# Attention with a routed feed-forward on one core: gathered blocks transposed six half rounds after their gather, the first ranking's steps behind the maximum, weights a round later

## The chip, the cores and the metric

The kernel runs on one core of a Trainium2 chip. The metric is device time in microseconds of that core for one execution. Four engines run side by side: TensorE (PE; its weight loads are PEld), VectorE (DVE), ScalarE (ACT) and GpSimd (POOL); the queue of SyncE (SP) issues most transfers. [...]

## What is computed

Chunked attention: q, k and v have 8 batches, 8 heads, 576 positions and 64 columns; every chunk of 64 positions attends to itself alone. The result, seen as 4608 rows of 512 columns, then goes through a mixture of experts in which only some rows take part, each with its best of 8 experts.

```
scores = scale * np.matmul(q_c, k_c.transpose(0, 1, 2, 4, 3))
scores = scores - np.max(scores, axis=-1, keepdims=True)
attn = np.exp(scores)
attn = attn / (np.sum(attn, axis=-1, keepdims=True) + 1e-09)
x = np.matmul(attn, v_c)                      # as rows of 512

do_compute = (x @ w_skip) > 0
logits = x[do_compute] @ w_gate               # 8 experts
e = argmax(logits);  gate = softmax(logits)[e]
h = np.maximum(x @ w1[e], 0.0)                # 512 -> 1024
out = x + gate * (h @ w2[e])                  # rows that take part; x elsewhere
```

## The kernel before

**Rounds.** The attention works on 36 tiles of 128 rows. One loop, `for i in range(-1, NT + 5)` (line 698), is a software pipeline; I call one pass of it a round and name it by i. Round i issues, in this order on TensorE: the transposes of the probabilities of tile i-1 (`pe_ptrans`, L259), the subtraction of the maximum of tile i (`pe_sub`, L248), the transposes of the attention result of tile i-3 (`pe_xtrans`, L297), a first share of feed-forward work (`fill`, half round 2i), the scores of tile i+1 (`pe_scores`, L237), the gate logits of tile i-4 (`pe_logits`, L322 and L323), the product with v of tile i-1 (`pe_pv`, L276), and a second share of feed-forward work (half round 2i+1). So the row of L237 with tile t belongs to round t-1, and the distance of two such rows is the length of a round.

DVE has in a round: the reduction of the logits (`ve_logits`, L332), the normalisation of tile i-2 (`ve_norm`, L282, L284, L286) and the maximum of tile i+1 (`ve_max`, L242, which waits for the scores of the same round). `pe_logits` writes into the same PSUM tile `pv` that `ve_norm` reads, so L322 of a round waits for L286 of that round. ACT has the exponential (L252), the copy of the transposed probabilities (L264) and the copy of the transposed result (L308); POOL splits that copy into a high and a low float16 part (L309, L312: two halves of 256 columns up to tile 14).

**Ranking.** The 36 tiles fall into five groups of 4, 8, 8, 7 and 9 tiles. When a group's logits are complete, `route(g)` (line 339) turns them into row numbers for each expert's blocks. It is a generator whose steps each carry a kind and a cost: "d" for DVE steps, "p" for the counting matmuls, "r" for reading their result, "w" a pause, "q" for the matmuls that collect the records. `run_route(kinds, budget)` (line 461) issues steps of the kinds named until the costs use the budget up. Line 729 does it ahead of `ve_max`, line 741 behind `pe_pv`. The first group alone (`early()`) has shares of 700 and 600; it fills blocks 0 to 2 of the first expert, 128 rows each. Its last steps are `finish_records` (L443 to L445), which yields the row numbers `reci`.

**Gather and filler.** `early_fetch(True)` then starts one gather a round (`gather`, L490, an indirect transfer that POOL issues, out of the rows that the stores have written to `out`). `filler()` (line 635) is a generator of the first expert's feed-forward on these three blocks: four transposes a block (L503), then layer 1 (L524) and layer 2 (L549), one step at a time. `fill(0.95)` in every half round takes a step if the generator gives one; it gives none until `is_open(m)`, that is until `F_LAG[m]` half rounds after block m's gather (5, 5, 4; 6 for the fourth). After the last tile, what is left of it is taken at once.

**Transfers by a table.** `EXTRAS` says in which round a store (`s`) or a piece of the first expert's weights (`w`, 256 KB) or of the second's (`r`, 512 KB) is issued on SP's queue; `CONV` in which round a piece of weights is split into float16 parts by ACT and POOL (L485 to L487). q, k and v of a tile are loaded about two to three rounds ahead. A tile's store must have landed before its slot of `hold` or `xb` is written again by L286. `more_constants` (line 209) prepares the gate's weights for L322; it stands behind round 3.

After the loop the other experts' blocks follow, unit by unit.

Of the kernel before, what the change touches and what calls it, by code (L numbers as in the profile page):

```python
# [14 lines left out]
ALU = mybir.AluOpType  # L15
# [28 lines left out]
EARLY_G, EARLY_B = 1, 3  # L44
# [5 lines left out]
RS = 5120  # L50
EMPTY = 5120.0

LOOK = 3
EXTRAS = {3: "- s0", 5: "s1", 7: "s2", 8: "s3", 11: "w0", 12: "w1", 13: "w2", 14: "w3", 15: "w4", 16: "w5 s4", 17: "w6 s5", 18: "w7 s6",
# [3 lines left out]
CONV = {i: "w" for i in range(14, 31) if i != 27} | {35: "r", 36: "r", 37: "r", 38: "r", 39: "r", 40: "rrr"}  # L58
HOLD, XB, H_LAST = 8, 6, 26
NPRE = 15  # L60
F_LAG = (5, 5, 4, 6)
F_RATE = 0.95
W_ORDER = tuple((fc, part) for part in range(2) for fc in range(FC))
WSETS = 3
# [43 lines left out]
def moe_attention_kernel(ctx: ExitStack, tc: tile.TileContext, q: bass.AP, k: bass.AP, v: bass.AP, cst: bass.AP, wall: bass.AP, out: bass.AP):  # L108
    nc = tc.nc
# [20 lines left out]
    xb = ap.tile([P, XB, DM], F32, name="xb", bufs=1)  # L130
    store_at = {int(u[1:]): i for i, us in EXTRAS.items() for u in us.split() if u[0] == "s"}
    slots, free_at = [], [-1] * (HOLD + XB)
# [10 lines left out]
    def paced(dma):  # L143
        if pe_last[0] is not None:
            ins, to = (getattr(x, "ins", x) for x in (dma, pe_last[0]))
            tc.add_manual_dep(ins, to.name, mybir.DependencyInfo(mybir.DependencyClass.Sync, mybir.DependencyReason.DATA), reason="transfers are spread over the iteration")

    def load_q(t):
        if t < NT:
            T[t]["qk"] = qkb[:, t % (LOOK + 1)]  # L150
            paced(nc.sync.dma_start(T[t]["qk"][:, 0], q[t]))

    def load_k(t, eng=None):
        if t < NT:
            paced((eng or nc.sync).dma_start(T[t]["qk"][:, 1], k[t]))

    def load_v(t):
        if t < NT:
            T[t]["v"] = vb[:, t % (LOOK + 1)]
            paced(nc.sync.dma_start(T[t]["v"], v[t]))  # L160
# [42 lines left out]
    addr = cpool.tile([P, NT], F32, name="addr")  # L203
# [5 lines left out]
    def more_constants():  # L209
        nc.scalar.activation(wgs[:, :, 0], wg, AF.Copy, scale=SR)  # L210
        nc.gpsimd.tensor_scalar(wg, wg, SR, 1.0, op0=ALU.mult, op1=ALU.mult)
        nc.gpsimd.tensor_tensor(wgs[:, :, 1], wg, wgs[:, :, 0], op=ALU.subtract)

    def row_constants():
        nc.scalar.activation(upper, C("upper"), AF.Copy)
        nc.scalar.activation(iota, C("iota"), AF.Copy)
        nc.gpsimd.tensor_copy(vals[:, :, 0], C("tok"))
        nc.gpsimd.tensor_copy(vals[:, :, 2], C("part").to_broadcast([P, NT]))
        nc.gpsimd.memset(ecum[:, 0, :], 0.0)
        nc.gpsimd.memset(rec, 0.0)  # L220
# [118 lines left out]
    def route(g):  # L339
        n, t0 = GS[g], sum(GS[:g])  # L340
# [16 lines left out]
        val = spool.tile([P, n], F32, name="val", bufs=2)  # L357
# [18 lines left out]
        w = f.stop - f.start  # L376
# [26 lines left out]
        rank = spool.tile([P, n], F32, name="rank", bufs=2)  # L403
        nc.vector.tensor_reduce(rank, ad, axis=AX.X, op=ALU.add)
        if g < CUT_G:
# [6 lines left out]
            yield "d", 100  # L412
            key = spool.tile([P, n], F32, name="key", bufs=2)
            nc.vector.scalar_tensor_tensor(key, val, -40.0, bi, op0=ALU.mult, op1=ALU.add)
        yield "d", 100
        nc.vector.scalar_tensor_tensor(addr[:, t0:t0 + n], val, -float(RS), rank, op0=ALU.mult, op1=ALU.add)
        if g >= CUT_G:
            return
        yield "d", 220
# [16 lines left out]
        nc.vector.tensor_tensor(rec, rec, rp.rearrange("p (z b) -> p z b", z=4), op=ALU.add)  # L436
        if g + 1 == EARLY_G:
            finish_records(0, EARLY_B)
        elif g + 1 == CUT_G:
            finish_records(EARLY_B, NB)  # L440

    def finish_records(lo, hi):
        nc.vector.scalar_tensor_tensor(reci[:, lo:hi], rec[:, 0, lo:hi], EMPTY, rec[:, 2, lo:hi], op0=ALU.add, op1=ALU.add)  # L443
        nc.vector.tensor_tensor(recg[:, lo:hi], rec[:, 1, lo:hi], rec[:, 3, lo:hi], op=ALU.add)  # L444
        nc.vector.tensor_scalar(recg[:, lo:hi], recg[:, lo:hi], 1.0 / (SGATE * SX * SW * SW), None, op0=ALU.mult)  # L445
        ready.append(hi)
# [5 lines left out]
    def late_group():  # L452
        return routes and routes[0][2] >= CUT_G

    def early():
        return routes and routes[0][2] < EARLY_G

    def urgent():
        return routes and routes[0][2] + 1 == CUT_G

    def run_route(kinds, budget):
        while routes and routes[0][0][0] in kinds and budget > 0:
            budget -= routes[0][0][1]
            held[0] = {"p": "p", "q": "q", "r": ""}.get(routes[0][0][0], held[0])
            routes[0][0] = next(routes[0][1], None)
            if routes[0][0] is None:
                routes.pop(0)
# [14 lines left out]
    def conv_half(w_pend):  # L482
        st, fc, r = w_pend.pop(0)
        w = w1x if r is None else wsets[0][:, :, :, r]
        nc.scalar.activation(w[:, 0, fc], st, AF.Copy, scale=SW)  # L485
        nc.gpsimd.tensor_scalar(st, st, SW, 1.0, op0=ALU.mult, op1=ALU.mult)
        nc.gpsimd.tensor_tensor(w[:, 1, fc], st, w[:, 0, fc], op=ALU.subtract)  # L487
# [75 lines left out]
    def on(f, t, *a):  # L563
        if 0 <= t < NT:
            f(t, *a)
# [21 lines left out]
    def early_fetch(mid=False):  # L587
        m = min([m for m in range(EARLY_B) if m not in xgs], default=EARLY_B)
        if m < EARLY_B and cur[0] % 2 == 0 and mid:
            fetch(m, EARLY_ROWS)  # L590
        if ready[-1] == NB:
            m = min([m for m in range(EARLY_B, XGB) if m not in xgs], default=XGB)
            if m < XGB:
                fetch(m, CUT_ROWS)
        for m in xgs:
            fetched.setdefault(m, cur[0])
# [31 lines left out]
    def is_open(m):  # L628
        return m in fetched and cur[0] >= fetched[m] + F_LAG[min(m, EARLY_B)]

# [42 lines left out]
    def fill(n):  # L673
        credit[0] += n
        while credit[0] >= 1 and next(fill_, False):
            credit[0] -= 1
        credit[0] = min(credit[0], 1)

    def flush(n=1 << 30):
        while late and n:  # L680
            f, *a = late.pop(0)
            f(*a)
            n -= 1
# [10 lines left out]
    def move(us):  # L694
        for u in us:
            {"-": int, "s": store, "w": load_half, "r": load_raw}[u[0]](int(u[1:] or 0))

    for i in range(-1, NT + 5):
        cur[0] = 2 * i
        extra = [u for u in EXTRAS.get(i, "").split()]  # L700
        if held[0]:
            run_route("d", 1 << 30)
        run_route("r", 1)
        run_route("w", 1)
        early_fetch()
        on(ve_logits, i - 5)
        on(ve_norm, i - 2)
        on(pe_ptrans, i - 1)
        if i < NPRE:
            on(ac_pt, i - 1)  # L710
        on(pe_sub, i)
        on(ac_exp, i)
        if i >= NPRE:
            on(ac_pt, i - 1)
        if i == 0 or i > 1:
            load_q(i + LOOK + (i == 0))
        on(pe_xtrans, i - 3)
        move(extra[2:])
        on(ac_xt, i - 3, i - 3 >= NT - 9)
        fill(F_RATE if i < NT else 2)  # L720
        if i == 0 or i > 1:
            load_k(i + LOOK + (i == 0))
        on(pe_scores, i + 1)
        if i == 1:
            paced(nc.sync.dma_start(csb, cst))
        move(extra[:1])
        if not urgent() and not early():
            run_route("q", 1)
        run_route("d", 600 if urgent() else 700 if early() else 350 if not late_group() else 0)
        on(ve_max, i + 1)  # L730
        flush()
        on(pe_logits, i - 4, i - 1 if i - 1 < NT else None)
        on(pe_pv, i - 1)
        for t in range(vnext[0], min(NT, i + LOOK) if i >= 0 else 0):
            load_v(t)
            vnext[0] = t + 1
        if urgent() or early():
            run_route("q", 1)
        if not late_group():
            run_route("p", 1)  # L740
        run_route("rd" if urgent() or early() else "d", 600 if urgent() or early() else 200 if not late_group() else 0)
        early_fetch(True)
        cur[0] = 2 * i + 1
        fill(F_RATE if i < NT else 2)
        if i == 3:
            more_constants()
        if i == 5:
            row_constants()
        move(extra[1:2])
        for u in CONV.get(i, ""):  # L750
            conv_half(w_pend if u == "w" else r_pend)
# [141 lines left out]
    for u, (p, bs, offs, n) in list(enumerate(units))[1:]:  # L893
# [10 lines left out]
        w, hc = wsets[p], ht  # L904
# [103 lines left out]
```

## Time and profile before

| what | us |
|---|---|
| median of 3 runs | 336.6 |
| the profiled execution's own time | 336.5 |
| its span, first to last instruction | 334.7 |
| PE busy | 314.5 |
| DVE busy | 235.4 |
| POOL busy | 153.9 |

A row of a timeline gives its start, its length, the engine, the line, what is written and read, and in brackets how long the engine had been idle and who ended that. A timeline merges neighbouring instructions of one line (x32 is 32 of them). A row of windows gives a stretch, its length, the busy time of each engine with the count of its instructions, the granted clock of TensorE, the busy share of the transfer engines and GB/s. Between span and time lie 1.8 us.

### The profile page before, as it was taken

How to read it: one execution, taken by the hardware profiler on the slowest of the kernel's cores; microseconds unless marked ns; L12 is line 12 of the kernel's file. 1: busy time of each engine (PE TensorE's matmuls, PEld its weight loads, DVE VectorE, ACT ScalarE, POOL GpSimd, SP SyncE). 2: the span in 40 equal slices, each digit the busy share in tenths (PEclk: the TensorE clock that was granted, in tenths of full speed). 3: DMA queues.
4: the chain of work that ended last, by engine and by line, in shares of the span. 5: the costliest groups of instructions: out<-in, count | busy, mean ns of one | idle time of the engine just before them, and what ended most of it. 6: DMA issues, size and time to landing. Idle time of an engine off the chain costs nothing. (4 is left out here: it accounts for less than half of the span.)

```text
span 334.7 us, 11279 instructions
## 1 busy us (share of the span) xinstructions
PE 314.5 (94%) x4537; PEld 221.8 (66%) x4537; DVE 235.4 (70%) x558; ACT 163.2 (49%) x340; POOL 153.9 (46%) x190
## 2 busy tenths in 40 slices
PE   7999896999999999999999999999999999999991
PEld 3777675777777777767555447647647649678580
DVE  1656763879478758955579876886887999868430
ACT  2555444655546543354557454554554555457120
POOL 5176685989979780358960451231232221120111
PEclk9999899999999999999999999999999999999997
DMA  7998889899999999969824787666667676754010
GB/s 258 340 316 277 282 247 354 263 301 303 307 318 291 348 388 364 379 213 343 289 65 125 255 307 226 208 209 227 192 220 253 194 224 233 243 172 154 34 30 28
DMA packets 41320, 81.83 MB, mean 245 GB/s; under 512 B 5022, under 2 KB 5022, under 8 KB 41264
## 3 DMA queue, kind: packets, MB, share of 16 engines
q1 hardware_dynamic: 38016, 71.48, 64.3%
q0 software_dynamic: 3104, 9.33, 8.6%
q8 instruction: 37, 0.61, 0.7%
q10 hardware_dynamic: 144, 0.26, 0.2%
q14 instruction: 19, 0.16, 0.1%
HBM read 67.02 MB, written 14.17 MB: 243 GB/s over the span
## 5 line engine op out<-in xcount | busy, mean ns | idle before, releaser
L549 PE MATMUL y<-wset,ht 128*128 128x512 f16 (+7 forms) x480 | 86.2, 380 | 0.0
L490 POOL DMA_INDIRECT out<-yo,reci x22 | 24.5, 1114 | 119.0 <-DVE yo L559 112.6
L524 PEld LDWEIGHTS <-wset 128*128 128x128 f16 x768 | 63.9, 98 | 14.5 <-issue 2.3
L549 PEld LDWEIGHTS <-ht 128*128 128x128 f16 (+7 forms) x552 | 44.8, 101 | 42.4 <-issue 2.0
L802 DVE SCALAR_TENSOR_TENSOR wset<-wst,wset 128x512 f16<-128x512 f32 x96 | 61.5, 683 | 0.8 <-ACT wset L801 0.4
L524 PE MATMUL hp<-xt,wset 128*128 128x288 f16 (+4 forms) x576 | 60.4, 267 | 0.0
L801 ACT ACTIVATE wset<-wst 128x512 f16<-128x512 f32 x96 | 53.9, 620 | 3.9 <-DVE wset L802 2.2
L528 ACT ACTIVATE ht<-hp 128x288 f16<-128x288 f32 (+5 forms) x56 | 21.7, 388 | 44.3 <-PE hp L524 44.1
L242 DVE TENSOR_REDUCE mx<-sp 128x8 bf16<-128x512 f32 x36 | 24.7, 687 | 24.9 <-PE sp L237 24.9
L252 ACT ACTIVATE px<-sp 128x512 f32<-128x512 f32 x36 | 21.4, 595 | 37.3 <-PE sp L248 29.1
L516 DVE SCALAR_TENSOR_TENSOR ht<-hp,ht 128x288 f16<-128x288 f32 (+5 forms) x56 | 23.6, 429 | 17.1 <-ACT ht L528 16.5
L312 POOL TENSOR_TENSOR xh<-xs,xh 128x256 f16<-128x256 f32 (+1 forms) x42 | 33.4, 811 | 2.2
L264 ACT ACTIVATE pts<-pt 128x512 f32<-128x512 f32 x36 | 21.4, 595 | 20.7 <-PE pt L259 20.7
L490 POOL DMA_INDIRECT xg<-out,reci x22 | 24.6, 1116 | 12.2 <-DVE recg L444 6.8
L237 PEld LDWEIGHTS sp<-qkb 64*64 64x64 f32 x1152 | 20.6, 136 | 11.4 <-ACT px L252 7.5
L276 PE MATMUL pv<-vb,pts 64*64 64x65 f32 x1152 | 26.4, 225 | 0.9 <-issue 0.8
L309 POOL CAST xh<-xs 128x512 f16<-128x512 f32 x27 | 16.8, 621 | 21.2 <-ACT xs L308 21.0
L237 PE MATMUL sp<-qkb 64*64 64x64 f32 x1152 | 25.7, 227 | 0.8 <-ACT px L252 0.6
L276 PEld LDWEIGHTS pv<-vb,pts 64*64 64x64 f32 x1152 | 21.1, 135 | 2.2 <-issue 1.4
L504 ACT ACTIVATE xt<-xq 128x512 f16<-128x512 f32 (+6 forms) x18 | 9.1, 511 | 27.6 <-PE xq L503 27.6
L259 PE MATMUL pt<-ident,px 128*128 128x128 f32 x144 | 22.4, 278 | 0.1
L559 DVE SCALAR_TENSOR_TENSOR yo<-y,recg,xg 128x512 f32<-128x512 f32 (+7 forms) x20 | 14.8, 741 | 7.6 <-PEq L944 5.0
(138 smaller groups left out, 463.9 us busy)
## 6 DMA issues: line engine op xcount, KB each, us to landing
wst<-in_wall SPq DMA_DIRECT2D x96, 256.0 KB, 3.9
vb<-in_v SPq DMA_DIRECT2D x36, 260.0 KB, 4.7
qkb<-in_q SPq DMA_DIRECT2D x36, 256.0 KB, 5.0
qkb<-in_k SPq DMA_DIRECT2D x35, 256.0 KB, 5.0
out<-hold SPq DMA_DIRECT2D x20, 256.0 KB, 5.2
wset<-in_wall SPq DMA_DIRECT2D x16, 256.0 KB, 5.2
out<-xb SPq DMA_DIRECT2D x16, 256.0 KB, 5.0
wset<-in_wall SPq DMA_DIRECT2D x8, 512.0 KB, 6.7
```

Of the source, the lines that this page charges most:

```text
L237: pe_last[0] = nc.tensor.matmul(sp[halves[a], c, j * CH:(j + 1) * CH], qk[halves[c], 0, w], qk[halves[c], 1, w], start=(j == 0), stop=Fals ...
L242: nc.vector.tensor_reduce(mx, T[t]["sp"][:, :, :KC * CH].rearrange("p c (j s) -> p c j s", s=CH), axis=AX.X, op=ALU.max, negate=True)
L259: pe_last[0] = nc.tensor.transpose(pt[:, j, :], px[:, j * P:(j + 1) * P], ident)
L276: pe_last[0] = nc.tensor.matmul(pv[halves[c], jj, m * VW:(m + 1) * VW], pt[halves[jj], c * 2 + jp, halves[a]], vv[halves[jj], c * KC + m, ...
L312: nc.gpsimd.tensor_tensor(xh[:, 1, w], xs[:, w], xh[:, 0, w], op=ALU.subtract)
L490: ins = nc.gpsimd.indirect_dma_start(**kw)
L516: nc.vector.scalar_tensor_tensor(ht[:, 1, fc, :n], hp, 0.0, ht[:, 0, fc, :n], op0=ALU.max, op1=ALU.subtract)
L524: pe_last[0] = nc.tensor.matmul(hp, w()[:, a, fc, j * P:(j + 1) * P], xt[:, b, j, :n], start=(m == 0), stop=(m == 11))
L528: nc.scalar.activation(ht[:, 0, fc, :n], hp, AF.Relu)
L549: pe_last[0] = nc.tensor.matmul(y[c * P // cg:c * P // cg + n], ht[:, a, fc, o:o + n], w[:, b, fc, P * KC:], start=(f == 0 and m == 0), st ...
L801: nc.scalar.activation(w[:, 0, fc, r], st[part], AF.Copy, scale=SW)
L802: nc.vector.scalar_tensor_tensor(w[:, 1, fc, r], st[part], SW, w[:, 0, fc, r], op0=ALU.mult, op1=ALU.subtract)
```

## The change

Four things. The three early blocks are transposed six half rounds behind their gather, where it was 5, 5 and 4. The first group's ranking gets no share ahead of the maximum any more; it gets 450 right behind it and 350 behind `pe_pv`, and the step that writes `addr` goes to the end, behind `finish_records`. The gate's weights are prepared behind round 2, not 3. The first expert's weights are loaded and split a round later, and some stores are put elsewhere in the table.

```
-EXTRAS = {3: "- s0", 5: "s1", 7: "s2", 8: "s3", 11: "w0", 12: "w1", 13: "w2", 14: "w3", 15: "w4", 16: "w5 s4", 17: "w6 s5", 18: "w7 s6",
...
+EXTRAS = {3: "- s0", 5: "s1", 7: "s2", 9: "s3", 12: "w0", 13: "w1", 14: "w2", 15: "w3", 16: "w4 s4", 17: "w5 s5", 18: "w6 s6", 19: "w7 s7",
...
-CONV = {i: "w" for i in range(14, 31) if i != 27} | {35: "r", 36: "r", 37: "r", 38: "r", 39: "r", 40: "rrr"}
+CONV = {i: "w" for i in range(15, 32) if i != 28} | {35: "r", 36: "r", 37: "r", 38: "r", 39: "r", 40: "rrr"}
...
-F_LAG = (5, 5, 4, 6)
+F_LAG = (6, 6, 6, 6)
...
-        yield "d", 100
-        nc.vector.scalar_tensor_tensor(addr[:, t0:t0 + n], val, -float(RS), rank, op0=ALU.mult, op1=ALU.add)
+        def address():
+            nc.vector.scalar_tensor_tensor(addr[:, t0:t0 + n], val, -float(RS), rank, op0=ALU.mult, op1=ALU.add)
+
+        if g + 1 != EARLY_G:
+            yield "d", 100
+            address()
...
         if g + 1 == EARLY_G:
             finish_records(0, EARLY_B)
+            yield "d", 100
+            address()
...
-        run_route("d", 600 if urgent() else 700 if early() else 350 if not late_group() else 0)
+        if not early():
+            run_route("d", 600 if urgent() else 350 if not late_group() else 0)
         on(ve_max, i + 1)
+        if early():
+            run_route("d", 450)
...
-        run_route("rd" if urgent() or early() else "d", 600 if urgent() or early() else 200 if not late_group() else 0)
+        run_route("rd" if urgent() or early() else "d", 600 if urgent() else 350 if early() else 200 if not late_group() else 0)
...
-        if i == 3:
+        if i == 2:
             more_constants()
```

On DVE, in round 8, where the first group's ranking begins, from the normalisation (L286) on; m, ex, eq, val, eh and es are the ranking's:

```order
 L286 TENSOR_TENSOR hold<-pv,rr 128x512
+L242 TENSOR_REDUCE mx<-sp 128x8
 L347 TENSOR_REDUCE m<-lg 128x4
 L350 TENSOR_TENSOR ex<-lg,m 128x32
```

```order
 L358 TENSOR_REDUCE val<-eq 128x4
 L360 SCALAR_TENSOR_TENSOR val<-lg,val 128x4
-L242 TENSOR_REDUCE mx<-sp 128x8
 L363 TENSOR_TENSOR eh<-csb,val 128x36
 L366 TENSOR_REDUCE es<-eh 128x9
```

The maximum moves from behind the first five steps to ahead of all seven.

On DVE, rounds 9 to 11 before the change, from the ranking's read of its counts (den, gate, rank, bi, sl, key, addr, ohb and oh are the ranking's):

```order
L392 TENSOR_REDUCE den<-pe 128x4
L397 RECIPROCAL gate<-den 128x4
L332 TENSOR_REDUCE lg<-pv 128x9
L282 TENSOR_SCALAR rs<-pv 128x8
L284 RECIPROCAL rr<-rs 128x8
L286 TENSOR_TENSOR hold<-pv,rr 128x512
L404 TENSOR_REDUCE rank<-ad 128x4
L408 TENSOR_SCALAR bi<-rank 128x4
L411 SCALAR_TENSOR_TENSOR sl<-bi,rank 128x4
L414 SCALAR_TENSOR_TENSOR key<-val,bi 128x4
L416 SCALAR_TENSOR_TENSOR addr<-val,rank 128x4
L421 TENSOR_TENSOR ohb<-csb,key 128x88
```

And the same place of the changed kernel:

```order
L392 TENSOR_REDUCE den<-pe 128x4
L332 TENSOR_REDUCE lg<-pv 128x9
L282 TENSOR_SCALAR rs<-pv 128x8
L284 RECIPROCAL rr<-rs 128x8
L286 TENSOR_TENSOR hold<-pv,rr 128x512
L242 TENSOR_REDUCE mx<-sp 128x8
L397 RECIPROCAL gate<-den 128x4
L404 TENSOR_REDUCE rank<-ad 128x4
L408 TENSOR_SCALAR bi<-rank 128x4
L411 SCALAR_TENSOR_TENSOR sl<-bi,rank 128x4
L414 SCALAR_TENSOR_TENSOR key<-val,bi 128x4
L425 TENSOR_TENSOR ohb<-csb,key 128x88
```

`gate`, which reads what POOL made of `den`, no longer stands ahead of the normalisation; `addr` has left this place.

On PE, rounds 14 to 16 (fb<-ident,xg are the transposes of a gathered block; L503 of before is L509 of the changed kernel); in round 13 one such row has gone as well:

```order
 L276 MATMUL pv<-vb,pts 64x65 x16
-L503 MATMUL fb<-ident,xg 128x128 x4
 L259 MATMUL pt<-ident,px 128x128 x4
 L248 LDWEIGHTS identb
```

```order
 L297 MATMUL xt<-ident,xb 128x128 x4
-L503 MATMUL fb<-ident,xg 128x128 x4
+L509 MATMUL fb<-ident,xg 128x128 x4
 L237 MATMUL sp<-qkb 64x64 x16
```

The three blocks were transposed in half rounds 27, 29 and 30; now it is 30, 32 and 34, always between L297 and L237. Layer 1 of the filler, which began in half round 31, begins in 35.

## Rows read from the trace of the kernel before

**Rows 1.** The page's busy times: engine, busy us, share of the span.

```profile
PE 314.5 (94%) x4537; PEld 221.8 (66%) x4537; DVE 235.4 (70%) x558; ACT 163.2 (49%) x340; POOL 153.9 (46%) x190
```

**Rows 2.** Windows: stretch, length, busy of the five engines, PEclk, DMA share, GB/s.

```profile
36.00:44.00 8.00, 6.60 (x162) 5.55 (x162) 6.07 (x19) 2.85 (x6) 5.04 (x11) 0.79 0.81 262
...
50.00:60.00 10.00, 6.86 (x164) 5.92 (x168) 3.59 (x9) 5.59 (x11) 6.44 (x9) 1.00 0.90 324
60.00:80.00 20.00, 19.39 (x447) 15.38 (x438) 17.67 (x50) 11.08 (x24) 17.54 (x24) 1.00 0.94 298
...
52.00:54.00 2.00, 1.37 (x48) 1.04 (x45) 0.17 (x1) 1.51 (x4) 0.88 (x2) 1.00 1.04 398
```

**Rows 3.** Timeline of PE, rounds 4 to 19: start, length, what, idle before.

```profile
18.08 0.17 PE L322 MATMUL pv<-wgs,xh 128*128 128x18 f16 x1 [0.52 <-POOL wgs L212]
...
30.08 0.69 PE L237 MATMUL sp<-qkb 64*64 64x64 f32 x32
32.87 0.69 PE L237 MATMUL sp<-qkb 64*64 64x64 f32 x32
33.50 0.18 PE L322 MATMUL pv<-wgs,xh 128*128 128x18 f16 x1
...
37.64 0.17 PE L322 MATMUL pv<-wgs,xh 128*128 128x18 f16 x1 [0.98 <-DVE hold L286]
39.94 0.58 PE L248 MATMUL sp<-mx,identb 128*128 128x256 bf16 x2 [0.35 <-DVE mx L242]
41.31 1.13 PE L237 MATMUL sp<-qkb 64*64 64x64 f32 x32
45.79 0.17 PE L322 MATMUL pv<-wgs,xh 128*128 128x18 f16 x1 [0.18 <-DVE hold L286]
50.72 0.63 PE L503 MATMUL fb<-ident,xg 128*128 128x128 f32 x4 [1.18 <-DMA xg<-out,reci]
53.07 0.69 PE L237 MATMUL sp<-qkb 64*64 64x64 f32 x32 [0.63 <-ACT px L252]
55.78 0.66 PE L503 MATMUL fb<-ident,xg 128*128 128x128 f32 x4 [1.10 <-DMA xg<-out,reci]
58.22 0.63 PE L503 MATMUL fb<-ident,xg 128*128 128x128 f32 x4 [0.69 <-DMA xg<-out,reci]
...
75.88 0.17 PE L322 MATMUL pv<-wgs,xh 128*128 128x18 f16 x1 [0.61 <-DVE hold L286]
```

**Rows 4.** Timeline of DVE, rounds 8 to 10, and one wait of round 19.

```profile
30.09 0.17 DVE L347 TENSOR_REDUCE m<-lg 128x4 f32<-128x32 f32 x1
31.05 0.68 DVE L242 TENSOR_REDUCE mx<-sp 128x8 bf16<-128x512 f32 x1
31.65 0.24 DVE L363 TENSOR_TENSOR eh<-csb,val 128x36 f16<-128x36 f32 x1
32.57 0.69 DVE L286 TENSOR_TENSOR hold<-pv,rr 128x512 f32<-128x512 f32 x1
36.31 0.18 DVE L397 RECIPROCAL gate<-den 128x4 f32<-128x4 f32 x1 [0.83 <-POOL den L394]
37.92 0.57 DVE L411 SCALAR_TENSOR_TENSOR sl<-bi,rank 128x4 f32<-128x4 int32 x1
38.42 0.15 DVE L414 SCALAR_TENSOR_TENSOR key<-val,bi 128x4 f32<-128x4 f32 x1
```

**Rows 5.** Timeline of POOL, rounds 8 to 14.

```profile
31.23 0.61 POOL L309 CAST xh<-xs 128x512 f16<-128x512 f32 x1 [1.93 <-ACT xs L308]
37.81 1.30 POOL L312 TENSOR_TENSOR xh<-xs,xh 128x256 f16<-128x256 f32 x2
44.65 1.27 POOL L490 DMA_INDIRECT xg<-out,reci  x1 [0.50 <-DVE recg L444]
48.22 1.04 POOL L490 DMA_INDIRECT xg<-out,reci  x1 [0.16 <-issue]
51.42 1.04 POOL L490 DMA_INDIRECT xg<-out,reci  x1 [0.15 <-issue]
```

4 rows, old and new, of the table EXTRAS are left out of this document.

## The prediction

> **What bounds the kernel now.** I read the page first: PE is busy 314.5 us of the span of 334.7 [rows 1], so a change can gain no more than PE's idle time and what PE loses to a lower clock. Then the windows, for where that is: from 60 to 80 us PE works 19.39 of 20 us, but from 36 to 44 only 6.60 of 8, at a granted clock of 0.79, and from 50 to 60 only 6.86 of 10 [rows 2]. The last stretch is rounds 14 and 15, the one before it rounds 10 and 11: just the rounds that hold the first ranking and the transposes of the three gathered blocks. Then PE's timeline, for who ends each wait [rows 3]. A quiet round is 2.79 us long (L237 at 30.08 and at 32.87). From round 10 on the waits that count are:
>
> - for DVE, in the ranking: 0.98 (L322 at 37.64), 0.35 (L248 at 39.94), 0.18 (L322 at 45.79), together 1.51;
> - for the gathers: 1.18, 1.10 and 0.69 at the three rows of L503, together 2.97;
> - for ACT's exponential: 0.63 (L237 at 53.07), where one PSUM bank serves two tiles in turn and ACT had the gathered block to copy first.
>
> [...] In all, 6.8 us can be had between rounds 10 and 16. After 60 us PE is full, so what is won here stays won: the filler's steps that come later take the same PE time there, and their number does not change.
>
> **The change part by part.** The sum is made against the profiled execution's 336.5 us, which is 0.1 under the median of the runs.
>
> *The 6.8 us of before go* (-6.8), all of them, as instructions now stand elsewhere; what takes their place follows, each with its own size.
>
> *Maximum ahead of the ranking, round 8.* No step is added or removed. Before, five small steps ran from 30.09 to 31.05, while DVE would have waited for the scores anyway, and only then the maximum; eh started at 31.65 and the normalisation behind it ended at 33.26, 1.61 us later [rows 4], in time for L322 at 33.50 [rows 3]. Now the maximum comes first. It can start about 0.77 us behind L237's start at 30.08 (an estimate: the scores' 0.69 us and a little), at 30.85, and takes 0.60 (31.05 to 31.65), so it ends at 31.45. Then come the five steps, 0.96 us, and the 1.61: the normalisation ends at 34.02, and L322 is 0.5 late. That is with no hindrance. But the five steps now fall on POOL's cast, which starts at 31.23, and the two halves behind it [rows 5]; before, POOL was idle until then. What this costs a step rows show: sl took 0.57 us and ended with POOL's first half, which began at 37.81, where key, a step of the same form, took 0.15 right behind it [rows 4, 5]. So a held step loses 0.42. Four of the seven steps read two operands from SBUF as sl does (ex, eq, the second val, eh). If two or three of them are held, L322 is late by 1.3 to 1.8; I take 1.5, with 0.5 and 1.8 as ends. [...]
>
> *Rounds 9 to 13.* gate no longer makes the normalisation wait for POOL's den, 0.83 us [rows 4]; that was most of the 0.98. Seven steps (gate, rank, bi, sl, key, ohb and, later, oh) stand behind the maximum of rounds 10 and 11, and DVE is behind when the logits come. With the durations of [rows 4] and one step held a round I get lateness of L322 of 0.2 (round 10), 0.35 (round 11), none in round 12 and 0.45 in round 13, where finish_records and addr now stand in POOL's busy part: 1.0 in all. Below, with nothing held, it is 0.5; above, it is what stood here before, 1.5.
>
> *The bank in round 14.* Without a transpose to fill the time, L237 of round 14 still needs the exponential of the same round: 0.63 before, of which the copy of a gathered block took about 0.3. I take 0.4 (0.3 to 0.63).
>
> *The gathers.* From POOL's issue to PE's first transpose it took 6.07, 7.56 and 6.80 us (50.72-44.65, 55.78-48.22, 58.22-51.42) [rows 3, 5], and PE was waiting each time, so these are landings. Half a round more is 1.4 us for the first two blocks, a whole one 2.8 for the third; but the rounds get shorter, so the time allowed is not simply longer. Walking on from the lateness above, with a round of 2.79 and 0.5 more where a block is transposed (0.63 a row, part of it overlapped): the first gather has some 6.5 us against 6.07, the second 6.4 to 6.6 against 7.56 at worst and 6.07 at best, the third 6.6 against 6.80. I take 0, 0.3 and 0.1, together 0.4. The ends are 0 and the 2.97 of before.
>
> *The loads.* Rounds 12 to 14 issue, by the shapes of their tiles, q, k and v (772 KB), a piece of weights (256) and a gather (256): 1.31 million bytes, at 3.0 us a round 440 GB/s, over the highest stretch that I find, 398 [rows 2]. At that rate such a round needs 3.3 us. The waits above lengthen these rounds to about that, so I add 0.2, with 0 and 1.5 as ends.
>
> *Weights a round later.* The same instructions on ACT, POOL and SP; the filler's layer 1 also starts two rounds later, so no piece is missed. One store (tile 4) is now issued in a round without a filler step behind it, and its slot is written two rounds on: like the 0.61 at 75.88, where the normalisation waited for a store to land [rows 3]. I take 0.2, ends 0 and 0.6.
>
> *Gate weights behind round 2.* L322 waited 0.52 for POOL's product at 18.08 [rows 3]. The split of the result, behind which POOL did it, ends shortly before, so about half stays: -0.25, with -0.52 as one end and 0.3 as the other, if ACT should wait for the constants to land.
>
> Sum: -6.8 + 1.5 + 1.0 + 0.4 + 0.4 + 0.2 + 0.2 - 0.25 = -3.35; 336.5 - 3.35 is 333.2 us.
>
> **The rivals.**
>
> *The clock falls all the same.* It fell after a wait of 0.98, and the new wait in round 9 is longer by my own reckoning. Against it: between 50 and 60 us three waits of that size left the clock at 1.00 [rows 2]. [...]
>
> *The gathers remain the wait.* Shorter rounds eat the later half round, landing gets slower with denser loads, and the 2.97 stay but for the first block's 1.18 or so: 1.8 instead of 0.4, 334.6. For it: landings of 6.07 to 7.56 while PE idled. Against: half a round more is allowed for the first two and a whole one for the third.
>
> *The loads become the bound.* q and k come too late in rounds 12 to 17, 1.5 instead of 0.2: 334.5. For it: 440 GB/s wanted; against: 398 was reached with a share of 1.04 and no wait for q or k is in the trace.
>
> *DVE has room.* No step is held, and nothing of the 6.8 comes back but the bank's 0.3 and the 0.5 of round 9: 336.5 - 6.8 - 0.25 + 0.8 = 330.2. The row of sl speaks against it.
>
> *Slower: ranking behind the maximum starves PE twice.* Mechanism: every step of two SBUF operands in rounds 8 to 13 is held by a POOL instruction, normalisations come late in each of them (1.8, then 0.7 a round for four rounds, 4.6), and the clock falls in two stretches, round 9 and rounds 11 to 12 (3.4), with gathers and bank as forecast (0.8). That is 8.8 against the 7.05 that go: 338.2. It decides once the DVE waits pass 2.9 with two falls of the clock. For it: POOL's cast and halves take 1.9 us of each round [rows 5]; against: single-operand steps between them let POOL pass.
>
> **How the numbers follow.** The forecast of 333.2 gets 0.45, the clock 0.24, the gathers 0.1, the loads 0.07, room on DVE 0.09, the slower case 0.05. The terms' own ends spread the forecast by about 1.5 to each side. So 8 in 10 lie between 329.9 (DVE with room, and the 0.52 of the gate weights won whole) and 336.3 (clock and gathers together, 333.2 + 1.7 + 1.4). A difference of 2%, 6.7 us, is about what a measurement of this kernel can tell from no change: below 329.8 lies only the better half of the case with room on DVE, 0.05; above 343.2 next to nothing, 0.02; within, 0.93.
>
> **What would show it.** Right: PE has a wait of over 1 us for the normalisation in round 9 that was not there, smaller ones in rounds 10 to 13, a wait of under 0.6 in sum at the three transposes, and a clock of 1.00 from 36 to 44 us; ex, eq or eh of round 8 take 0.4 and more. L237 of round 14, at 53.07 before [rows 3], comes at about 50.3, by the same walk. Wrong: the clock at 0.5 somewhere before 60 us (the first rival), waits of the transposes for xg over 1.5 (the second), L237 waiting for q or k (the third), or a first idle time of PE after 60 us that the kernel before does not have.

## The result, and the profile after

The changed kernel took 339.33 us (median of 20 runs) where the kernel before took 336.45 (20 runs) beside it: a ratio of 1.0094, 95% interval 1.0067 to 1.0121. Ratios here and below leave out the few slow runs (over 1.5% above the fastest at a lower granted clock, as 344.87 and 343.37 of these 20) and are not the quotients of the medians (1.0086 for these). It is slower, by about 3 us, and not 3 us faster; 333.2 had been forecast, and 336.3 was the upper end of the range. It lies within the 2% for which 0.93 had stood. The profiled execution took 341.17 us, 1.8 over the median; its span is 339.3. The page's row for the engines, beside [rows 1]:

```profile
PE 316.4 (93%) x4537; PEld 223.1 (66%) x4537; DVE 237.2 (70%) x558; ACT 163.4 (48%) x340; POOL 153.9 (45%) x190
```

The windows of the changed kernel show where the clock went; columns as in [rows 2]:

```profile
36.00:44.00 8.00, 7.28 (x186) 6.21 (x189) 7.38 (x25) 3.83 (x8) 5.32 (x10) 1.00 0.80 226
50.00:60.00 10.00, 6.51 (x107) 5.36 (x109) 2.30 (x6) 3.40 (x7) 7.57 (x10) 0.68 0.77 262
53.62:60.46 6.84, 5.85 (x86) 5.06 (x86) 1.14 (x4) 2.42 (x5) 6.08 (x10) 0.50 0.63 200
60.00:80.00 20.00, 19.47 (x481) 15.94 (x476) 17.62 (x50) 12.24 (x25) 17.88 (x24) 0.99 0.93 313
```

From 36 to 44 us the clock is whole now, as forecast. But from 50 to 60 it is 0.68 on average, where it had been 1.00: one stretch, the 6.8 us of the third row, lies at the lower level, 0.50, throughout, twice as long as the 3.4 us at 0.50 in the kernel before:

```profile
39.82:43.22 3.40, 3.28 (x66) 2.75 (x69) 2.61 (x7) 1.66 (x3) 1.30 (x3) 0.50 0.76 217
```

Now PE's timeline of the changed kernel, from 28 us to round 15 and two places much later (start, length, what, idle before):

```profile
28.19 0.57 PE L276 MATMUL pv<-vb,pts 64*64 64x65 f32 x21 [0.99 <-issue]
...
33.67 0.56 PE L237 MATMUL sp<-qkb 64*64 64x64 f32 x19 [0.50 <-issue]
34.69 0.17 PE L322 MATMUL pv<-wgs,xh 128*128 128x18 f16 x1 [0.46 <-DVE hold L286]
...
41.67 0.17 PE L322 MATMUL pv<-wgs,xh 128*128 128x18 f16 x1 [0.28 <-POOL rv L428]
...
51.01 0.69 PE L237 MATMUL sp<-qkb 64*64 64x64 f32 x32 [0.58 <-ACT px L252]
53.71 0.19 PE L322 MATMUL pv<-wgs,xh 128*128 128x18 f16 x1 [2.01 <-POOL xh L309]
54.46 0.19 PE L323 MATMUL pv<-wgs,xh 128*128 128x9 f16 x1 [0.56 <-POOL xh L312]
...
55.08 0.19 PE L323 MATMUL pv<-wgs,xh 128*128 128x9 f16 x1 [0.35 <-POOL xh L312]
...
58.52 1.06 PE L509 MATMUL fb<-ident,xg 128*128 128x128 f32 x4
59.51 1.10 PE L237 MATMUL sp<-qkb 64*64 64x64 f32 x32
...
118.74 0.47 PE L438 MATMUL xt<-rv,oh 128*128 128x88 f16 x8 [0.95 <-POOL rv L428]
...
132.21 0.17 PE L322 MATMUL pv<-wgs,xh 128*128 128x18 f16 x1 [0.75 <-DVE xb L286]
```

The three waits for gathered blocks, 2.97 us in [rows 3], are gone: the first transpose, at 58.52, follows on PE's work, and so do the other two. The wait of 0.52 for the gate weights at 18.08 is gone as well. L237 of round 14 starts at 51.01 instead of 53.07, 2.1 us earlier. Then, in that same round, come 2.01 + 0.56 + 0.35 = 2.92 us of waits for POOL's cast and halves, and the next L237 comes at 59.51, 0.7 us later than the 58.78 of before. POOL's timeline says why the cast was late:

```profile
45.65 1.30 POOL L312 TENSOR_TENSOR xh<-xs,xh 128x256 f16<-128x256 f32 x2
51.74 1.27 POOL L496 DMA_INDIRECT xg<-out,reci  x1 [4.79 <-issue]
53.03 0.62 POOL L309 CAST xh<-xs 128x512 f16<-128x512 f32 x1
```

POOL is free at 46.96 and starts its first gather at 51.74: 4.79 us of idle time that ended on nothing the profile shows ("issue"). Before, the same gather started 0.50 behind POOL's earlier work [rows 5]. What it waits for by its semaphores was there: its block's index (reci) at 46.34, the stores long before. The cast is queued behind it. One thing that moves inside this gap can be seen, in the view of the DMA queues from 49.4 to 50.1 us (packets, MB, share):

```profile
q1 hardware_dynamic: 134, 0.25, 94.1%
q14 instruction: 1, 0.01, 2.8%
```

A block of 8 KB on an instruction queue (q14). Then PE's idle time, summed over the trace from one L237 to the next:

| stretch, by the start of L237 (before / after) | idle before | idle after |
|---|---|---|
| start to 30.08 / 29.93 (round 8) | 4.31 | 3.90 |
| to 58.78 / 59.51 (round 15) | 5.17 | 5.96 |
| to 116.98 / 117.10 (round 29) | 1.44 | 1.58 |
| to the end | 2.29 | 4.31 |

That is 2.5 us more; the lower clock, at 0.50, costs by my estimate half of 6.8 instead of half of 3.4, 1.7 more; together 4.2 of the 4.6 by which the spans differ (339.3 against 334.7). The last row of the table holds the two waits at 118.74 (0.95, for rv, the product of the third group's ranking, which the expectations below call the second) and at 132.21 (0.75, for the normalisation), which the kernel before does not have.

The same sums by what ended the waits read otherwise. PE's waits of over 0.25 us that end on nothing shown, like those at 28.19 and 33.67, add up to 0.8 us in the kernel before and to 3.5 in the changed one; all its other idle time is 12.4 and 12.3. In two further profiles of the changed kernel such waits are 2.0 and 1.7 us. So two profiles alone do not tell what the change costs: the new waits in round 14 and behind 60 us stand against those that are gone, and what each is worth is for the experiments to say. What they are is taken up at the end.

### The profile page after: what moved, and what is told of

The parts are those of the page before. It is cut to its first block, busy times and chain, and to the rows that moved or that the text cites. A ratio compares the mean times of both kernels' runs of the same rounds, so it can differ in the third digit from the quotient of the medians.

```text
span 339.3 us, 11274 instructions
## 1 busy us (share of the span) xinstructions
PE 316.4 (93%) x4537; PEld 223.1 (66%) x4537; DVE 237.2 (70%) x558; ACT 163.4 (48%) x340; POOL 153.9 (45%) x190
## 5 line engine op out<-in xcount | busy, mean ns | idle before, releaser
L312 POOL TENSOR_TENSOR xh<-xs,xh 128x256 f16<-128x256 f32 (+1 forms) x42 | 34.3, 831 | 2.2
L496 POOL DMA_INDIRECT xg<-out,reci x22 | 23.9, 1088 | 10.4 <-issue 9.1
L237 PEld LDWEIGHTS sp<-qkb 64*64 64x64 f32 x1152 | 20.8, 137 | 11.7 <-ACT px L252 6.3
L237 PE MATMUL sp<-qkb 64*64 64x64 f32 x1152 | 26.0, 227 | 1.4 <-issue 0.8
L259 PE MATMUL pt<-ident,px 128*128 128x128 f32 x144 | 23.1, 284 | 0.1
```

The source lines that it names most:

```text
L237: pe_last[0] = nc.tensor.matmul(sp[halves[a], c, j * CH:(j + 1) * CH], qk[halves[c], 0, w], qk[halves[c], 1, w], start=(j == 0), stop=Fals ...
L259: pe_last[0] = nc.tensor.transpose(pt[:, j, :], px[:, j * P:(j + 1) * P], ident)
L312: nc.gpsimd.tensor_tensor(xh[:, 1, w], xs[:, w], xh[:, 0, w], op=ALU.subtract)
L496: ins = nc.gpsimd.indirect_dma_start(**kw)
```

## The experiments

The kernels of each group below ran on one chip, with the kernel before beside them; its median was 336.3 us for the first group and 339.2 and 339.1 for the others, so sizes are compared as ratios within a group.

**Does the place in POOL's stream make the stand?** The edit, put into both kernels, gives POOL four more instructions at the very start, which touch nothing else:

```
     nc.gpsimd.tensor_copy(identb, ident)
+    for _z in range(4):
+        nc.gpsimd.memset(cpool.tile([P, 1], F32, name="idle%d" % _z), 0.0)
```

and the opposite one, in the changed kernel, gives half of an old group of fills to DVE:

```
-    for _ in range(XGB):
-        nc.gpsimd.memset(spool.tile([P, DM], F32, name="xg", bufs=XGB), 0.0)
+    for _z in range(XGB):
+        (nc.gpsimd if _z < 4 else nc.vector).memset(spool.tile([P, DM], F32, name="xg", bufs=XGB), 0.0)
```

> The changed kernel once more, as the measure for the runs beside it. The trace of the changed kernel shows POOL standing 4.8 us ahead of the first gather (51.74 us) with its semaphores long given; the next cast is queued behind that gather, PE waits 2.92 us for it in round 14 and the clock is at its lower level from 53.6 to 60.5 us. Theory P (the stand depends on where the gather stands in POOL's stream of instructions, since a block of 8 KB on the instruction queue moves just then) and theory R (it comes from the work at that time: transfers, DVE, stores) both expect the same again: a stand of 4 to 5 us, PE waiting 2.5 to 3.2 us in round 14, and 338 to 340 us.

> The changed kernel with four tiny fills on POOL at the very start, so that every later POOL instruction stands four places further down its stream; nothing else differs at 47 us. Theory P: the block is fetched at another place, the first gather starts within 0.6 us of POOL's earlier work, PE's 2.9 us wait in round 14 and the fall of the clock from 53.6 to 60.5 us are gone: 2.9 + 3.4 less, about 333 to 335 us (another place may be held instead, where it may cost less). Theory R: as the changed kernel, stand of 4 to 5 us, within 0.3% of it.

> The kernel before with the same four tiny fills, so that its first gather has the place in POOL's stream that it has in the changed kernel. Theory P: the first gather, which started 0.5 us behind POOL's earlier work, now stands 4 to 5 us; the casts behind it come late, PE waits 2 to 3 us in rounds 11 or 12 and the time rises by 2 to 6 us. Theory R: no change, within 0.3% of the kernel before.

> The changed kernel with four of the eight fills of the gather's buffers moved from POOL to DVE at the start, so that POOL's stream is four instructions shorter, as long as in the kernel before when the first gather comes. Theory P: the first gather starts within 0.6 us of POOL's earlier work as in the kernel before, no wait of 2.9 us in round 14 and no fall of the clock there: 333 to 335 us. Theory R: as the changed kernel, within 0.3% (the fills at the start cost less than 0.5 either way).

Measured, as ratio to the kernel before: the changed kernel again 1.0104 (1.0009 to 1.0198), with the fills 1.0041 (0.9993 to 1.0088), with four fewer 1.0024 (0.9981 to 1.0066), and the kernel before with the fills 1.0057 (1.0019 to 1.0094). POOL in the changed kernel with the fills:

```profile
46.62 1.31 POOL L314 TENSOR_TENSOR xh<-xs,xh 128x256 f16<-128x256 f32 x2
48.10 1.28 POOL L498 DMA_INDIRECT xg<-out,reci  x1 [0.18 <-issue]
49.39 0.62 POOL L311 CAST xh<-xs 128x512 f16<-128x512 f32 x1
```

and in the kernel before with the same fills:

```profile
43.80 1.30 POOL L314 TENSOR_TENSOR xh<-xs,xh 128x256 f16<-128x256 f32 x2
47.91 1.27 POOL L492 DMA_INDIRECT xg<-out,reci  x1 [2.80 <-DVE mx L244]
49.19 0.62 POOL L311 CAST xh<-xs 128x512 f16<-128x512 f32 x1
```

The stand (POOL idle ahead of the first gather with its semaphores given) left the one and came into the other, 0.18 against 2.80 us. (The releaser named in the second, a maximum, is only what ended last on DVE; the gather does not read it.) In the changed kernel run again it was 3.94, with four fewer instructions 0.18. Counted in the traces, with the records of POOL's own queue that the timeline leaves out, the gather has 68 POOL instructions ahead of it wherever there is a stand (the changed kernel and the kernel before with fills), and 64 or 72 wherever there is none. Theory P holds, in both directions; R, which wanted no effect of instructions at the start, falls. In the kernel before with fills PE pays for the late casts 1.30 us, in round 13 (2 to 3 us in rounds 11 or 12 had been expected), and then 2.13 at the first transpose, which had been 1.18:

```profile
49.87 0.18 PE L324 MATMUL pv<-wgs,xh 128*128 128x18 f16 x1 [0.37 <-POOL xh L311]
50.62 0.18 PE L325 MATMUL pv<-wgs,xh 128*128 128x9 f16 x1 [0.56 <-POOL xh L314]
...
51.24 0.18 PE L325 MATMUL pv<-wgs,xh 128*128 128x9 f16 x1 [0.37 <-POOL xh L314]
...
54.23 0.63 PE L505 MATMUL fb<-ident,xg 128*128 128x128 f32 x4 [2.13 <-DMA xg<-out,reci]
```

The price by the ratios is 0.6 to 0.8% in the changed kernel (1.0104 against 1.0041 and 1.0024; with four runs of the changed kernel these intervals overlap), 0.6% in the other (1.8 us, a little under the 2 to 6 expected; 1.0019 is the lower end): some 2 us. The expectation of 333 to 335 us for the kernels without the stand failed: they came out at 338.7 and 338.0, so more was wrong than the stand.

**The parts one by one.** First the changed kernel without the stand and with the tables EXTRAS and CONV of before; on the other side the kernel before with one part alone: the later weights (the two tables), the later transposes, or the new ranking (with the fills, which keep the gather from place 68). The edits are those of the diff ahead of the prediction; for the transposes:

```
-F_LAG = (5, 5, 4, 6)
+F_LAG = (6, 6, 6, 6)
```

> The changed kernel without POOL's stand (the four tiny fills at the start) and with the two tables of the weights as before; ranking, transposes and gate weights as changed. Theory W (the later weights put a conversion of 2.2 us on POOL in front of the second ranking's product and behind it into DVE's steps): PE's waits of 0.94 us at the second ranking (for rv, near 114 us) and of 0.75 us (near 128 us) are gone, the filler starts a round earlier, and the time is 1.5 to 2 us less than with the fills alone (338.7), about 337. Rival (these waits come from the ranking or from the filler that starts later): both waits stay and the time is within 0.2% of 338.7.

> The kernel before with the later weights alone. Theory W: the two waits, 0.9 us near 115 us (rv) and 0.75 us near 129 us (normalisation), appear here too, the two waits for a store of 0.6 to 0.8 us (75.9 and 93.3 us) may go; all in all 0.5 to 1.7 us slower than the kernel before. Rival: no such waits, within 0.3 us. The first gather stands where it stood, so POOL has no stand.

> The kernel before with the transposes of the first three gathered blocks six half rounds behind their gather, alone. Theory T (that part does what it says): PE's three waits for the gathered blocks, 2.97 us in sum, fall to under 0.7, and the time by about 2.3 us, to 334. Rival (the wait only moves): another wait of 1 us and more stands in rounds 14 to 16, for the bank (exponential) or for a cast, and the time falls by under 0.7 us.

> The kernel before with the new order and shares of the first ranking and the later address, with the four tiny fills that keep POOL's stand away. Theory K (the ranking's steps behind the maximum make the normalisation late): a wait of 1.0 to 1.3 us in round 9, waits of 0.3 to 1.0 in round 11 and 0.8 in round 13 for 1.5 us of waits before, so PE waits 0.5 to 1.5 us more than before, and the time rises by that to 337 to 338. Rival (the new order is the gain that was meant): PE waits under 1.5 us for DVE in rounds 8 to 13, the clock does not fall, and the time falls by 1 to 2 us.

Ratios: old weights in the changed kernel 0.992 (0.9882 to 0.9958), later weights alone 0.9984 (0.9945 to 1.0022), later transposes alone 0.9941 (0.9899 to 0.9983), new ranking alone 0.9993 (0.9958 to 1.0029).

- *Transposes.* T holds in mechanism: no wait for a gathered block is left in that kernel, and no wait for the bank or a cast takes its place. There is one of 1.47 us at 61.68, in round 16, that ends on nothing shown; it is of the kind taken up at the end. The gain is 0.6%, 2.0 us (0.2 to 1.0%), for 2.3 expected and 2.97 of waits that went.
- *Ranking.* The places that K named are there: 1.12 us at 38.25 in round 9 (named for POOL's cast, not for DVE), 1.04 for rv at 45.23 and 0.78 at 51.77 (named for nothing). But the time did not rise; by the interval the part is worth between -0.4 and +0.3%. Neither K's rise nor the rival's gain of 1 to 2 us at its upper end is borne out; the size of this part stays open.
- *Weights.* With the old tables the waits at the third group's ranking and at the normalisation behind it are gone, as theory W wanted; but the filler did not start a round earlier, as I had written: its first step stays where it is in the changed kernel, so the two rounds' delay is not due to the weights. And the same tables alone in the kernel before do not bring these waits, but others (PE's timeline of that kernel):

```profile
115.20 0.47 PE L434 MATMUL xt<-rv,oh 128*128 128x88 f16 x8 [0.20 <-POOL rv L424]
...
127.51 0.59 PE L549 MATMUL fb<-wset,ht 128*128 128x512 f16 x2 [0.66 <-POOL wset L487]
```

There rv costs 0.20, and the filler waits 0.66 for a converted piece. W as I wrote it falls in that half: the later tables cost this much only together with another part of the change, and I take the later filler for it. The rounds' starts in the traces fit that: of the two rounds ahead of the one with the wait for rv, the first is 3.44 us long in the changed kernel (L237 at 109.62 and 113.06), in the kernel before 4.17 and in this one 4.04, the second 4.0 in all three, and POOL has less time for the same work ahead of rv. Neither this reason nor which other part it takes was tried by itself.

**All on one chip.** The changed kernel, without the stand, without stand and later weights; and, as another way to the same gain, the kernel before with the later transposes and the gate weights behind round 2 only:

```
-F_LAG = (5, 5, 4, 6)
+F_LAG = (6, 6, 6, 6)
...
-        if i == 3:
+        if i == 2:
             more_constants()
```

> The changed kernel, on one chip with the three kernels beside it. Theory P (the first gather is POOL's 68th instruction, and there it waits for a block of instructions): a stand of 3 to 5 us ahead of the first gather, block about 2.1 us before the gather starts, ratio to the kernel before 1.008 to 1.012. Rival (a chance of the earlier chips): ratio under 1.004.

> The changed kernel with the four tiny fills. Theory P: no stand, ratio to the kernel before 1.001 to 1.005, some 0.4 to 0.8% under the changed kernel beside it; theory W: the waits of 0.94 us (rv, second ranking) and 0.75 us (normalisation) of the later weights stay. Rival to P (the stand is given back later, since another wait takes its place): within 0.2% of the changed kernel.

> The same with the tables of the weights as before. Theory W: both waits gone, 0.4 to 1.2% under the kernel with the fills alone beside it, ratio to the kernel before 0.990 to 0.997. Rival (the difference of the two earlier jobs was one of chips): within 0.3% of the kernel with the fills alone.

> The kernel before with two parts of the change, the later transposes and the gate weights behind round 2; ranking and weights as before. Theory T with K (the transposes are the gain, the new ranking is worth nothing or costs): the wait of 0.5 us for the gate weights at 18 us is gone, the transposes' waits are under 0.7 us, ratio 0.989 to 0.996, not over that of the kernel beside it with the new ranking by more than 0.2%. Rival (the new ranking adds to the gain): over 0.3% slower than that kernel.

| kernel | median us | ratio to before (95%) |
|---|---|---|
| changed | 340.31 | 1.0033 (0.9999 to 1.0067) |
| changed, four fills | 338.81 | 0.9959 (0.9928 to 0.9991) |
| changed, four fills, old weights | 335.82 | 0.9914 (0.9874 to 0.9955) |
| before, later transposes, gate weights | 337.57 | 0.9937 (0.9901 to 0.9973) |

The stand is worth 0.74% here, 2.5 us, and the two intervals do not overlap; the later weights are worth 0.45%, 1.5 us, with intervals that do overlap. The first step agrees with the first group, the second with the two waits, 0.93 + 0.76 = 1.69 us. The changed kernel itself did better than I expected against the kernel before (1.0033 where 1.008 to 1.012 stood; by the number alone the rival, under 1.004, was right, but the stand was there): in its profile here the stand was 2.64 us, under the 3 to 5 expected, and PE waited only 0.48 + 0.37 for the halves in round 14, and 0.85 for the first gathered block. The kernel before with two parts has no wait at the transposes and none for the gate weights, as T wanted. PE at the third group's ranking and the later normalisation with the fills alone,

```profile
112.72 0.47 PE L440 MATMUL xt<-rv,oh 128*128 128x88 f16 x8 [0.93 <-POOL rv L430]
...
126.20 0.17 PE L324 MATMUL pv<-wgs,xh 128*128 128x18 f16 x1 [0.76 <-DVE xb L288]
```

and at the ranking with the old weights as well (no wait at the normalisation is left there):

```profile
113.32 0.49 PE L440 MATMUL xt<-rv,oh 128*128 128x88 f16 x8 [0.19 <-ACT xs L310]
```

POOL in the profile of the changed kernel, before rv, shows how the first wait comes about:

```profile
112.84 0.71 POOL L492 TENSOR_SCALAR wset<-wset 128x512 f32<-128x512 f32 x1
113.63 1.48 POOL L493 TENSOR_TENSOR wset<-wset 128x512 f16<-128x512 f32 x1
115.05 1.07 POOL L309 CAST xh<-xs 128x512 f16<-128x512 f32 x1
116.20 1.16 POOL L312 TENSOR_TENSOR xh<-xs,xh 128x512 f16<-128x512 f32 x1
117.32 1.37 POOL L428 TENSOR_TENSOR rv<-ohb,vals 128x704 f16<-128x704 f16 x1
```

The conversion of weights (L492, L493) stands ahead of cast, halves and rv, without a gap. With the old tables it stands behind rv (POOL of the kernel with fills and old weights):

```profile
109.79 1.67 POOL L314 TENSOR_TENSOR xh<-xs,xh 128x512 f16<-128x512 f32 x1
111.43 1.35 POOL L430 TENSOR_TENSOR rv<-ohb,vals 128x704 f16<-128x704 f16 x1
112.87 0.62 POOL L494 TENSOR_SCALAR wset<-wset 128x512 f32<-128x512 f32 x1
```

The second wait comes of steps held as sl was in [rows 4] (0.57 where key took 0.15), at a place for which the prediction has no term. DVE of the changed kernel, and POOL beside it:

```profile
129.23 0.51 DVE L360 SCALAR_TENSOR_TENSOR val<-lg,val 128x7 f32<-128x7 f32 x1
...
130.35 0.69 DVE L367 TENSOR_TENSOR ecum<-ecum,es 128x9 f16<-128x9 f16 x1
```

```profile
129.11 0.62 POOL L492 TENSOR_SCALAR wset<-wset 128x512 f32<-128x512 f32 x1 [3.17 <-ACT wset L491]
129.81 1.20 POOL L493 TENSOR_TENSOR wset<-wset 128x512 f16<-128x512 f32 x1
```

val and ecum, steps of 0.15 and 0.17 us with the old tables, take 0.51 and 0.69 and end with POOL's two instructions (129.74 and 131.04 against 129.73 and 131.01), just ahead of the normalisation. The same two steps in the kernel before:

```profile
128.19 0.16 DVE L360 SCALAR_TENSOR_TENSOR val<-lg,val 128x7 f32<-128x7 f32 x1
...
128.96 0.17 DVE L367 TENSOR_TENSOR ecum<-ecum,es 128x9 f16<-128x9 f16 x1
```

The best kernel is the changed one with four fills and the old weights, 0.9% under the kernel before; the kernel before with transposes and gate weights alone, 0.6% under it, is not told apart from it by these intervals. So whether the new ranking adds anything stays open.

## Why the prediction was wrong, step by step

*The gathers, "I take 0, 0.3 and 0.1".* The price of waits at the transposes was right (none in the profile; 0.60, 0.72 and three times none in the five others of this family without the stand). The step that failed stands beside it: I took POOL's issue of the first gather to come as promptly as before, and had no term for its start. It came 4.79 us late, cost 2.92 us in round 14 and had a fall of the clock behind it. The experiments put 2 to 2.5 us of time on it, in this kernel and, with the stand put into it, in the kernel before.

*"All of the 6.8 us go", the clock.* The 6.8 are the 5.11 of the waits listed there (1.51 + 2.97 + 0.63) and 1.7 for the clock. No run shows the 1.7 as time by itself; the trace of before shows the clock at 0.50 for 3.4 us, a mean of 0.79 from 36 to 44 [rows 2], and 8 x 0.21 = 1.7 is my estimate of the loss. It stands in the range again as the clock's. The old stretch at the lower level went; a new one of 6.8 us at 0.50 came amid the new wait, by the same estimate 3.4 lost instead of 1.7. That is my first rival's sign (the clock at 0.5 somewhere before 60 us), but not by its cause: it named the new wait in round 9, and behind that the clock stayed whole in this profile. In two others with that wait it did fall there: a stretch of 3.4 us at the lower level began at 36.8 in the changed kernel run again and at 38.0 with four fewer instructions, behind waits of 1.28 us; with the fills the wait was 1.29 and the clock stayed whole. In further profiles such a stretch began at 19.7, 30.9 or 57.5 us, or none came before the end, so a fall at one place in one profile is a weak basis for a term of 1.7.

*"After 60 us PE is full, so what is won here stays won", and weights a round later, "0.2".* This failed by its second half. PE was full there in the kernel before; the later conversions, with the later filler, made two new waits of 1.7 us, the last of the signs that I had named. I had said that the same instructions stand on ACT, POOL and SP, and had not asked what each then stands in front of. The store's slot, the part that I did price, shows nothing in this profile, and the 0.61 at 75.88 is gone; three of the other profiles have 0.56 to 0.95 at that place.

*Round 8 and 9, 1.5.* PE waited 0.46 and before it 0.50 for nothing that is shown; in seven other profiles with the new ranking the wait in round 9 is 0.9 to 1.3, in one there is none. The mechanism is there, and 1.5 was over what any of them shows. I had reckoned with two or three held steps at 0.42 each; DVE and, below it, POOL:

```profile
31.30 0.18 DVE L347 TENSOR_REDUCE m<-lg 128x4 f32<-128x32 f32 x1
31.52 0.22 DVE L350 TENSOR_TENSOR ex<-lg,m 128x32 f32<-128x32 f32 x1
31.77 0.19 DVE L355 SCALAR_TENSOR_TENSOR eq<-ex,csb 128x32 f32<-128x32 f32 x1
32.00 0.18 DVE L358 TENSOR_REDUCE val<-eq 128x4 f32<-128x32 f32 x1
32.22 0.29 DVE L360 SCALAR_TENSOR_TENSOR val<-lg,val 128x4 f32<-128x4 f32 x1
32.55 0.63 DVE L363 TENSOR_TENSOR eh<-csb,val 128x36 f16<-128x36 f32 x1
```

```profile
31.08 0.61 POOL L309 CAST xh<-xs 128x512 f16<-128x512 f32 x1 [2.10 <-ACT xs L308]
31.77 1.35 POOL L312 TENSOR_TENSOR xh<-xs,xh 128x256 f16<-128x256 f32 x2
```

POOL's cast ends at 31.70, its two halves in the trace at 32.50 and 33.13. ex, val and eh end at 31.74, 32.52 and 33.18, just behind one of them each; eq, which began with the first half, takes 0.19 as before. So three steps are held, but here a held step loses only what is left of POOL's instruction when it begins: eh 0.39 (0.63 where it took 0.24 in [rows 4]), val some 0.1, ex next to nothing. The count was right and the price of each too high. The two steps of one operand, m and the first val, took 0.18 each beside POOL's cast and first half, where they had taken 0.17 and 0.19 with POOL idle.

*Rounds 9 to 13, 1.0.* 0.28 in round 11 (41.67, for rv) and 0.79 in round 13 (48.22): 1.07, right in sum. That the sum fits is luck: no wait for DVE in round 10 for 0.2, round 11's for POOL and not for the normalisation, and 0.79 in round 13 for 0.45. *The bank, 0.4:* 0.58 at 51.01, inside its ends. *L237 of round 14 at 50.3:* 51.01. *Gate weights, -0.25:* the whole 0.52 went here; in several other runs 0.25 for POOL's halves took its place, half, as forecast. *Loads:* no L237 waits for q or k in this profile; 0.63 and 0.22 in one other, at 17 and 34 us, ahead of the rounds that the term was for.

Taken together: the changed kernel without stand and with the old weights comes out as the sum had it. 333.2 over 336.5 is 0.990; it measured 0.992 and 0.9914. That is the sum as a whole; single terms missed on both sides, as told above. The two terms that the sum lacked, the stand (0.7%) and the weights behind 60 us (0.5%), lead from there to the 1.0033 of the third group. In the comparison that counts the ratio is 1.0094, 0.6% more; there the stand was 4.79 us in the profile and not 2.64, but that this makes the rest is not shown. The slower rival (DVE starving PE twice) named the right sign by a mechanism that did not come.

## What to carry to other kernels

A change of order shifts every instruction behind it in its engine's stream, and a stand like POOL's may hang on the place alone (4.79 us in the changed kernel, 0.18 with four fills); before an order is thought bad, shift the stream by a few idle instructions and measure again. For every step that is moved, ask what it now stands in front of in each later stage, not only whether the stage as a whole has room. And change order, lag and tables one at a time: here a gain of 0.9% lay hidden in a loss.

## What the hardware showed that I had not expected

POOL stood 2.6 to 4.8 us ahead of an indirect DMA whose semaphores were given, in all four profiles in which it had 68 POOL instructions ahead of it, and 0.2 to 0.5 us in the other ten. In all four the 8 KB block on the instruction queue began to move 2.0 to 2.1 us before the gather started (49.68 and 51.74 in the profile above); with 64 instructions ahead it moved 0.9 to 1.4 us behind the gather's start, with 72 over 4 us before it. What makes the stand longer or shorter is ahead of the block: it began to move 0.6 to 2.7 us after POOL was free, and why so late stays open. That the gather waits for that block fits all fourteen.

PE's waits that end on nothing shown say the same of another engine. Of 60 such waits of over 0.25 us from 9 us on, in all fourteen profiles, 53 stand at the 193rd or 194th place behind a multiple of 256 in PE's stream (weight loads, matmuls and the queue's own records counted in the trace), and 52 of the 53 end 2.2 to 2.9 us after a block of 16 KB began to move on the other instruction queue (q8). The wait of 0.99 at 28.19 is one; its block began at 25.89 (window 25.8 to 26.0):

```profile
q8 instruction: 1, 0.02, 29.7%
```

The 0.50 at 33.67, the 0.44 at 38.95 and the 1.47 at 61.68 with the later transposes alone stand at such places too. So PE and POOL seem both to wait now and then for their next instructions, and for PE it was 0.8 to 4.2 us a profile; no experiment moved PE's places, so that this is the cause is inferred. The packets on q8 have 16 KB here (37 with 0.61 MB in the changed kernel's profile), those on q14 8 KB (19 with 0.16 MB).
